# Summing a21 + a22 in two transfers, and moving four second-layer steps, in a Mamba-2 + ELU kernel

## The chip, the cores and the metric

The kernel runs on one core of a Trainium2 chip. The metric is the time of one execution on the device, in microseconds (us). A core has a matrix engine (TensorE, PE in the profile; PEld is its loading of weights), a vector engine (VectorE, DVE), a scalar engine (ScalarE, ACT), GpSimd (POOL) and a queue that issues transfers (SyncE, SP). Each runs its own list of instructions in order, and they wait for one another by semaphores. Transfers (DMAs) are issued by SP, ACT or POOL and run beside the engines. TensorE writes its products to PSUM, eight banks; DVE and ACT read them there.

## What is computed

A Mamba-2 scan over x (4 batches, 8 heads, 768 tokens, head dimension 32; state 16), and behind it a two-layer network with ELU, over 4 x 768 = 3072 tokens of 8 x 32 = 256 features:

```python
for c in range(nc):                       # chunks of tokens
    L = np.exp(cum[..., :, None] - cum[..., None, :]) * causal
    y_intra = np.einsum('bhij,bhjd->bhid', CB * L, xc)
    y_inter = np.einsum('bhin,bhnd->bhid', Cc, state) * decay_to_i[..., None]
    y[:, :, sl] = y_intra + y_inter
    state = decay_full[..., None, None] * state + np.sum(Bx, axis=2)
...
x = attn_out.transpose(0, 2, 1, 3).reshape(3072, 256)
h = x @ w_in                              # w_in 256 x 2048
g = np.where(h > 0, h, np.exp(np.minimum(h, 0)) - 1)
return g @ w_out                          # w_out 2048 x 256
```

The weights come as 64-bit floats, and the kernel turns them into 32-bit ones on the chip.

## The kernel before

**Tiles.** The tokens are cut into twelve blocks n = 0 to 11 of 256 tokens, taken in pairs (n, n + 1), so that a first-layer matmul has 512 columns. While the network runs on one pair, the scan of the next pair is put between its matmuls. The order on every engine is the one in which the program is written.

**First layer.** For the pairs from n = 2 on (n = 2 for its second half alone) `l1_words` (L778) computes a group m = 0 to 15 of 128 of the 2048 hidden features. It makes six matmuls in two PSUM banks, `high` and `both`. ACT then scales `both` (L796), DVE joins the two (L799), ACT takes the two functions of ELU (L805, L806), and DVE writes g with `end_words` (L813), which is called one group later. For every even m a subtraction on POOL follows. `high` is free only behind L813, `both` behind L796. `words_of_w` (L732) and `low_of_w` (L742) make from piece p of w_in the factors that groups 2p and 2p + 1 multiply by: the first on ACT and DVE, the second by two subtractions on POOL.

**Second layer.** The first blocks, 0 and 1, multiply plainly (`l2`, L825, matmuls at L832): step j reads the rows 2j and 2j + 1 (of 128 features) of w_out. From the pair 2 on, `second` (L871) multiplies two blocks together by seven products for four (the scheme of Strassen and Winograd). For this the features of w_out are taken in twos, even and odd, and its columns in two halves: a11, a12 (the even and the odd rows, columns 0 to 127), a21 and a22 (the same, columns 128 to 255) are views of w_out, each with eight rows i. Four sums of them are made beforehand: s1 = a21 + a22 in place of a21, and s2, s3, s4 in `s_out`. `less` (L709) writes the negative of a view on ACT, `plus` (L713) adds one to another by an adding transfer, which POOL issues (L715). The sum at issue is s1, written over a21, and it can start only when `l2` has read the last of a21.

`second(n)` is a generator. It goes twice (`half` 0 and 1, rows i = 0 to 3 and 4 to 7 of each view) through the seven products with a11, a12, s1, s2, s3, a22, s4, each of four *steps*, one row i a step, so that steps 0 to 27 are half 0 and steps 28 to 55 half 1. The k-th product of all fourteen goes into the one bank of the pool `p_o` if k is even, and into one of the seven banks of the pool `p_a` if it is odd; `p_a` also holds the first layer's and the scan's products. Behind the last step of a product ACT or DVE read it and free the bank: behind step 3 (a11) ACT copies it to p1 (L919), behind step 19 (s3) DVE adds it twice and ACT copies it to c12 (L944), behind step 27 (s4) DVE subtracts (L959). Behind step 31 DVE makes three adds (L885) and POOL four subtractions.

**The first pair with `second`.** The loop at L1309 begins with n = 4: its sixteen groups k are each followed by some scan work (`stage_scan`) and by a number of steps of `second(2)`, by a table at L1331:

```python
l2s((3 + (n == 4), 3 - (n == 4), 3, 3, 3, 3, 3, 3, 4, 5, 2, 2, 3, 1, 1, 0)[k])
```

So for n = 4 the groups 0 to 9 have 4, 2, 3, 3, 3, 3, 3, 3, 4 and 5 steps behind them. Steps 8 (the first with s1) and 24 (the first with s4) are the last of group 2 and the first of group 8. Behind the steps of group 9 come `scores` (L545, four banks of `p_a`), `sums` (L575, two banks), on DVE the weighing of the scores (L554), and two more steps; then `states` (DVE and POOL). Ahead of this loop, at L1277, stand the last preparations of w_in and w_out.

Of the kernel before, what the change touches and what calls it, by code (L numbers as in the profile page):

```python
# [14 lines left out]
ALU = mybir.AluOpType  # L15
# [17 lines left out]
def kernel(  # L33
# [27 lines left out]
    nc = tc.nc  # L61
# [30 lines left out]
    for k in range(4):  # L92
        (nc.scalar if k % 2 else nc.sync).dma_start(
            out=la0[BH * k:BH * (k + 1)],
            in_=a.rearrange("b h (c s) -> (b h) c s", s=P)[:, 0:2, :])
# [187 lines left out]
    for v in range(2):  # L283
        nc.gpsimd.affine_select(
            out=low16[Q * v:Q * v + Q], in_=low16[Q * v:Q * v + Q], pattern=[[1, Q]],
# [5 lines left out]
        out=hmask, in_=hmask, pattern=[[-N, NH]], compare_op=ALU.is_ge, fill=0.0,  # L291
        base=0, channel_multiplier=1)
    nc.gpsimd.affine_select(
        out=hmask, in_=hmask, pattern=[[N, NH]], compare_op=ALU.is_ge, fill=0.0,
# [8 lines left out]
        out=minus, in0=ident, scalar1=-1.0, scalar2=None, op0=ALU.mult)  # L303
# [213 lines left out]
    def decay(n, q):  # L517

        decay_of(n, 2 * q)
        decay_of(n, 2 * q + 1)  # L520
# [15 lines left out]
    def scores(*ns):  # L536

        gs = [psum([P, len(ns), 2, 2, Q], "ps_g") for _ in range(4)]
        for at, n in enumerate(ns):
            s = st[n]  # L540
            for u in range(2):
                for v in range(2):
                    for q in range(4):
                        rows, toks = slice(32 * q, 32 * q + 32), slice(Q * v, Q * v + Q)
                        nc.tensor.matmul(  # L545
                            out=gs[q][toks, at, u], lhsT=s["bt"][rows, u, toks],
                            rhs=s["ctm"][rows, u, :, toks], start=True, stop=True,
                            tile_position=(32 * q, Q * v), skip_group_check=True)
            s["g"], s["M"] = [g[:, at] for g in gs], []
# [160 lines left out]

        nc.scalar.activation(out, in_, ACT.Copy, scale=-1.0)

    def plus(out, in_):  # L713

        nc.gpsimd.dma_start(out=out, in_=in_, accum_op=ALU.add)  # L715

    def weight_sums():
        return [conv.tile([P, MC // 2, P], F32, tag="w64", name="w_sum", bufs=W_AHEAD)
# [3 lines left out]
    a_out = [w_parts[:, k, r] for r in range(2) for k in range(2)]  # L722
# [19 lines left out]
    def low_of_w(i):  # L742

        w0 = conv.tile([P, KC, CW], F32R, tag="w_in", name="w0", bufs=DF // CW + 1)
        for k in range(KC):
            sub(w0[:, k], pieces[i][0][:, k], k_words[i][:, 0, k].bitcast(F32))
        k_words[i] = k_words[i], w0
# [20 lines left out]
    def both_of_y(n):  # L768
        y = yT[n // 2].rearrange("p k b u i -> p k (b u i)")
        y1, y0 = y_words[n]  # L770
        both = ffn.tile([P, KC, 2 * BLK], F32R, tag="yT", name="y_both")
        for k in range(KC):
            nc.vector.scalar_tensor_tensor(
                out=both[:, k], in0=y1[:, k].bitcast(F32), scalar=1.0 - WORD,
                in1=y[:, k], op0=ALU.mult, op1=ALU.add)
        y_words[n] = y1, y0, both

    def l1_words(n, m, between=None):  # L778

        cols = slice(m % 2 * P, (m % 2 + 1) * P)  # L780
        w, w0 = k_words[m // 2]
        w1, both_w, w0 = w[:, 0, :, cols], w[:, 1, :, cols], w0[:, :, cols]
        y1, y0, both_y = y_words[n]
        high, both = psum([P, 2 * BLK], "ps_h"), psum([P, 2 * BLK], "ps_w")
        passes = [(high, w1, y1), (high, w0, y0), (both, both_w, both_y)]
        for ps, lhs, rhs in passes if m == (8 if n == 2 else 0) or m == 15 else passes[2:] + passes[:2]:
            for k in range(KC):
                nc.tensor.matmul(  # L788
                    out=ps, lhsT=lhs[:, k], rhs=rhs[:, k], start=k == 0 and lhs is not w0,
                    stop=k == KC - 1 and lhs is not w1)  # L790
        if between:
            words_of_y(between)
            if between == 4:
                both_of_y(4)
        e = ffn.tile([P, 2 * BLK], F32, tag="e", name="e", bufs=2)
        nc.scalar.activation(e, both, ACT.Copy, scale=WORD)  # L796
        if late:
            end_words()
        nc.vector.scalar_tensor_tensor(  # L799
            out=high, in0=high, scalar=WORD - 1.0, in1=e, op0=ALU.mult, op1=ALU.add)  # L800
        late.append((n, m, high, e))

    def begin_end():
        high, e = late[-1][2:]
        nc.scalar.activation(e, high, ACT.Relu, scale=-1.0)  # L805
        nc.scalar.activation(e, e, ACT.Exp, scale=-1.0)  # L806
# [3 lines left out]
    def end_words():  # L810
        n, m, h, e = late.pop(0)
        g_of[n, m] = ffn.tile([P, 2, BLK], F32, tag=f"g{m % 2}", name="g", bufs=12)
        nc.vector.scalar_tensor_tensor(  # L813
            out=g_of[n, m].rearrange("p b i -> p (b i)"), in0=e, scalar=1.0, in1=h,
            op0=ALU.subtract, op1=ALU.max)
        if m % 2 == 0 and (n, m) != (2, 14):
            sub(g_of[n, m][:, 1], g_of[n, m][:, 1], g_of[n, m][:, 0])
# [29 lines left out]
    def sub(out, in0, in1):  # L847
        nc.gpsimd.tensor_tensor(out=out, in0=in0, in1=in1, op=ALU.subtract)  # L848
# [113 lines left out]
    def store(n, at):  # L962
        r0 = row_of(n + at)
        nc.sync.dma_start(
            out=out[r0:r0 + BLK, :].rearrange("(t p) e -> p t e", p=P),
            in_=c_of[n][:, at].rearrange("p t e c -> p t (e c)"))
# [173 lines left out]
    def weigh_two(m, q):  # L1140
        weigh(m, q)
        weigh(m + 1, q)
# [17 lines left out]
    def turn_step(n, k, late):  # L1160
        m = n + 2
        if m == NP or k > 7:
            return
        if m == 6:
            steps = [(6, 2), (7, 0), None, (7, 1), None, (7, 2), (6, 3), (7, 3)]
            if steps[k // 2 * 2 + late]:
                turn_part(*steps[k // 2 * 2 + late])
        else:
            at = k // 2 * 2 + late
            turn_part(*[(m, 0), (m, 1), (m, 2), (m + 1, 0), (m + 1, 1), (m + 1, 2), (m, 3), (m + 1, 3)][at])  # L1170

    for j in range(2 * DIRECT):
        n, i = 2 + j // DIRECT, j % DIRECT
# [47 lines left out]
        if j == 6:  # L1221
            less(s_out[1], a_out[2])
            plus(s_out[1], a_out[0])
# [3 lines left out]
    for j in range(8, 16):  # L1227
# [46 lines left out]
        if i == 2:  # L1274
            less(s_out[0], s_out[1])
            plus(s_out[0], a_out[3])
    end_words()  # L1277
    for p in (1, 2):
        low_of_w(p)
    plus(a_out[2], a_out[3])  # L1280
    plus(s_out[2], a_out[1])
    words_of_w(3)
    decay(6, 0)
# [4 lines left out]
    def stage_scan(n, k):  # L1288

        m = n + 2  # L1290
        if k < 2:
            spread_exp(m + k)
        if k == 2:
            load_x(m)
            load_x(m + 1)
        heads = ((5 + 3 * k) // 2, (8 + 3 * k) // 2) if n == 4 else (2 * k - 2, 2 * k)
        for h in range(*heads) if 0 < k < 9 else ():
            decay_of(m + h // NH, h % NH)
        if k == 7:
            scaled(m, nc.gpsimd)  # L1300
            scaled(m + 1, nc.gpsimd)
        if k in (6, 7) and m + 2 < NP:
            load_bc(m + k - 4)
        if k == 10 and m + 2 < NP:
            for to in (m + 2, m + 3):
                load_b(to)
                spread_cum(to)

    for n in range(4, NP, 2):  # L1309
        m = n + 2 if n + 2 < NP else None  # L1310
        steps = second(n - 2)

        def l2s(count):
            for _ in range(count):
                next(steps)

        for k in range(16):
            l1_words(n, k, between=m if k == 15 else None)
            turn_step(n, k // 2 * 2 + 1, k % 2)
            if n == 4 and k == 0:  # L1320
                decay(6, 1)
            if m:
                stage_scan(n, k)
            begin_end()
            if k == 0 and n > 4:
                store(n - 4, 0)
                store(n - 4, 1)
            if not m:
                l2s(4 if k % 2 else 3)
                continue  # L1330
            l2s((3 + (n == 4), 3 - (n == 4), 3, 3, 3, 3, 3, 3, 4, 5, 2, 2, 3, 1, 1, 0)[k])  # L1331
            if k == 9:
                scores(m, m + 1)
                sums(m, m + 1)
                for q in range(4):
                    weigh_two(m, q)
                l2s(2)
                states(m)
            if k == 10:
                states(m + 1)  # L1340
            if k == 13:
                y = across(m, m + 1)
                inside(y, m, m + 1, ts=(0,))
                l2s(4)
                inside(y, m, m + 1, ts=(1,))
        if m:
            l2s(4)
            both_of_y(m)
        end_words()
        for _ in steps:  # L1350
            pass
    n = NP - 2
# [34 lines left out]
```

## Time and profile before

| | us |
|---|---|
| median of three runs | 349.99 (348.40 to 350.48) |
| the profiled execution | 349.12 |
| its span, first to last instruction | 347.4 |
| mean granted TensorE clock | 1.000 |

The profile shows one execution. A line of a timeline gives the start, the time taken, the engine, the line of the kernel, the operation, the tile written and the tiles read, their shapes, how many instructions were merged, and in brackets how long the engine idled before it and what ended that. A line of the waits gives who waited for whom, the sum in us, how often, and the longest. A line of the stretches gives from and to, the length, the busy time and number of instructions of PE, PEld, DVE, ACT and POOL, the granted clock, the share of the DMA engines and GB/s. Matmuls overlap and their ends are modelled, so that a row of them may reach past the start of the next.

### The profile page before, as it was taken

To read this page: it belongs to the slowest core of one execution; us is meant where nothing else is said; L and a number is where in the kernel's file an instruction comes from. 1 tells how busy PE (TensorE), PEld (TensorE's weight loads), DVE (VectorE), ACT (ScalarE), POOL (GpSimd) and SP (SyncE) were. 2 spreads that over 40 slices of the span, in tenths; PEclk is the share of its full clock that TensorE was granted. 3 is DMA by queue.
4 is the path that set the end of the run, shared out by engine and by line. 5 is a ranking of instruction groups with operands and counts; after the bars stand their busy time and mean duration, and the time that the engine had idled before them with its cause. 6 is when DMAs were issued, how large, how long until landed. Compare 5 with 4: busy or idle time off the path is not lost.

```text
span 347.4 us, 9861 instructions
## 1 busy us (share of the span) xinstructions
PE 340.3 (98%) x3878; PEld 298.2 (86%) x3878; DVE 253.7 (73%) x504; ACT 237.8 (68%) x541; POOL 214.2 (62%) x320
## 2 busy tenths in 40 slices
PE   8999999999999999999999999999999999999996
PEld 5669888888788889888999988989988999999996
DVE  3898988879898778875878675878675766665232
ACT  4789989599758898657699447699457566565000
POOL 5553554559987798864296764196754264455760
PEclk9999999999999999999999999999999999999999
DMA  8898998371793891070431070320000100001001
GB/s 149 219 232 167 312 193 222 78 145 44 117 153 68 121 142 43 10 160 4 106 62 32 10 159 5 101 37 3 2 0 4 63 0 3 0 2 58 4 1 61
DMA packets 76887, 28.58 MB, mean 82 GB/s; under 512 B 57833, under 2 KB 71721, under 8 KB 76841
## 3 DMA queue, kind: packets, MB, share of 16 engines
q1 hardware_dynamic: 70360, 25.60, 31.9%
q0 software_dynamic: 4160, 2.10, 5.6%
q8 instruction: 30, 0.49, 0.7%
q10 hardware_dynamic: 2320, 0.26, 0.5%
q14 instruction: 17, 0.13, 0.1%
HBM read 22.51 MB, written 3.34 MB: 74 GB/s over the span
## 4 chain that ended last, share of the span: by engine, by line
PE 78%; DMA 5%; ACT 5%; DVE 5%; SPq 3%; issue 2%; POOL 1%; DVEq 0%; POOLq 0%; ACTq 0%
PE ps_o L907 32%; PE ps_h L788 15%; PE ps_h L671 11%; PE ps_w L788 8%; PE ps_o L832 5%; DMA w_out<-w_out 3%; PE ps_y L638 2%; DMA w<-in_moe_w_in_dram 2%; DVE ps_h L799 1%; PE ps_g L545 1%; PE ps_y L620 1%; ACT e L806 1%; ACT e L805 1%; SPq L148 1%; PE ps_st L575 1%
## 5 line engine op out<-in xcount | busy, mean ns | idle before, releaser
L907 PEld LDWEIGHTS ps_o<-w_out,g 128*128 128x128 f32 x640 | 78.6, 191 | 4.4 <-ACT e L796 1.0
L907 PE MATMUL ps_o<-w_out,g 128*128 128x128 f32 x640 | 80.3, 275 | 0.8 <-DMA w_out<-w_out 0.8
L805 ACT ACTIVATE e<-ps_h 128x512 f32<-128x512 f32 x72 | 43.0, 597 | 50.0 <-DVE ps_h L799 50.0
L813 DVE SCALAR_TENSOR_TENSOR g<-e,ps_h 128x512 f32<-128x512 f32 x72 | 49.3, 685 | 34.3 <-ACT e L806 33.9
L848 POOL TENSOR_TENSOR g<-g 128x256 f32<-128x256 f32 x36 | 28.4, 789 | 56.4 <-DVE g L813 56.1
L799 DVE SCALAR_TENSOR_TENSOR ps_h<-ps_h,e 128x512 f32<-128x512 f32 x72 | 50.1, 695 | 13.5 <-ACT e L796 10.6
L796 ACT ACTIVATE e<-ps_w 128x512 f32<-128x512 f32 x72 | 42.2, 586 | 13.7 <-PE ps_w L788 13.6
L788 PE MATMUL ps_w<-y_both,w_words 128*128 128x512 f32 x144 | 51.0, 434 | 0.0
L806 ACT ACTIVATE e<-e 128x512 f32<-128x512 f32 x72 | 45.5, 632 | 2.3
L671 PE MATMUL ps_h<-yT,w_in 128*128 128x256 f32 (+1 forms) x208 | 45.2, 368 | 1.4 <-POOL w_in L252 1.3
L788 PE MATMUL ps_h<-y,w_words 128*128 128x512 f32 x144 | 46.2, 402 | 0.0
L788 PE MATMUL ps_h<-y,w 128*128 128x512 f32 x144 | 44.8, 392 | 0.0
L671 PEld LDWEIGHTS ps_h<-yT,w_in 128*128 128x128 f32 x208 | 36.3, 190 | 7.5 <-POOL w_in L252 2.8
L525 ACT ACTIVATE L<-L,ncum 128x64 f32<-128x64 f32 x160 | 42.2, 336 | 0.2
L907 PE MATMUL ps_o<-w_sum,g 128*128 128x128 f32 x304 | 38.3, 275 | 0.0
L907 PEld LDWEIGHTS ps_o<-w_sum,g 128*128 128x128 f32 x304 | 37.1, 192 | 1.1
L530 POOL TENSOR_SCALAR_AFFINE_SELECT L<-L 64x512 f32<-64x512 f32 x40 | 29.6, 741 | 10.0 <-ACT L L525 8.6
L788 PEld LDWEIGHTS ps_h<-y,w 128*128 128x128 f32 x144 | 27.0, 188 | 6.7 <-POOL w L848 0.2
L848 POOL TENSOR_TENSOR g<-t,g 128x256 f32<-128x256 f32 x40 | 28.0, 734 | 5.8 <-PE ps_o L907 5.7
L788 PEld LDWEIGHTS ps_h<-y,w_words 128*128 128x128 f32 x144 | 26.4, 188 | 5.7 <-issue 0.4
L832 PE MATMUL ps_o<-w_out,g 128*128 128x256 f32 x128 | 31.0, 384 | 0.0
L848 POOL TENSOR_TENSOR t<-g 128x256 f32<-128x256 f32 x40 | 29.0, 757 | 0.2
(131 smaller groups left out, 536.0 us busy)
## 6 DMA issues: line engine op xcount, KB each, us to landing
L<-flat SPq DMA_DIRECT2D x20, 256.0 KB
w<-in_moe_w_out_dram SPq DMA_DIRECT2D x8, 512.0 KB
w<-in_moe_w_in_dram SPq DMA_DIRECT2D x7, 512.0 KB
xr<-in_x_dram SPq DMA_DIRECT2D x24, 128.0 KB
out_dram<-c_sum SPq DMA_DIRECT2D x9, 256.0 KB
bc<-in_B_dram SPq DMA_DIRECT2D x24, 64.0 KB
w_sum<-w_out POOLq DMA_DIRECT2D x3, 512.0 KB, 9.4
bc<-in_C_dram SPq DMA_DIRECT2D x22, 64.0 KB
```

The lines of the kernel that those rows point to most:

```text
L525: nc.scalar.activation(L[:, h, u], L[:, h, u], ACT.Exp, bias=ncum[:, u, row:row + 1])
L530: nc.gpsimd.affine_select(out=part, in_=part, pattern=[[0, 4], [0, 2], [1, Q]], compare_op=ALU.is_ge, fill=0.0, base=0, channel_multiplier=-1)
L671: nc.tensor.matmul(out=ps[:, j, toks], lhsT=w_in[i][:, k, j * P:(j + 1) * P], rhs=yT[n // 2][:, k, n % 2].rearrange("p u i -> p (u i)")[:, ...
L788: nc.tensor.matmul(out=ps, lhsT=lhs[:, k], rhs=rhs[:, k], start=k == 0 and lhs is not w0, stop=k == KC - 1 and lhs is not w1)
L796: nc.scalar.activation(e, both, ACT.Copy, scale=WORD)
L799: nc.vector.scalar_tensor_tensor(out=high, in0=high, scalar=WORD - 1.0, in1=e, op0=ALU.mult, op1=ALU.add)
L805: nc.scalar.activation(e, high, ACT.Relu, scale=-1.0)
L806: nc.scalar.activation(e, e, ACT.Exp, scale=-1.0)
L813: nc.vector.scalar_tensor_tensor(out=g_of[n, m].rearrange("p b i -> p (b i)"), in0=e, scalar=1.0, in1=h, op0=ALU.subtract, op1=ALU.max)
L832: nc.tensor.matmul(out=o_of[n][:, ts], lhsT=g_of[n, j][:, m % 2, ts * P:(ts + 1) * P], rhs=w_out[:, m], start=(m == 0 and ts == 0), stop=( ...
L848: nc.gpsimd.tensor_tensor(out=out, in0=in0, in1=in1, op=ALU.subtract)
L907: nc.tensor.matmul(out=ps[:, ts], lhsT=b[:, ts * P:(ts + 1) * P], rhs=a[:, i], start=(i == chunk[0] and ts == 0), stop=(i == chunk[-1]), s ...
```

## The change

The one transfer for s1 becomes two, over rows 0 to 3 and over rows 4 to 7 of the views. The first is issued between `low_of_w(1)` and `low_of_w(2)`, the second behind `low_of_w(2)`, where the whole one stood. And in the table of steps, for n = 4 alone, group 8 gets eight steps instead of four and group 9 one instead of five: steps 28 to 31 now come ahead of group 9's passes.

```diff
-    def plus(out, in_):
+    def plus(out, in_, rows=slice(None)):
 
-        nc.gpsimd.dma_start(out=out, in_=in_, accum_op=ALU.add)
+        nc.gpsimd.dma_start(out=out[:, rows], in_=in_[:, rows], accum_op=ALU.add)
...
     end_words()
-    for p in (1, 2):
-        low_of_w(p)
-    plus(a_out[2], a_out[3])
+    low_of_w(1)
+    plus(a_out[2], a_out[3], slice(0, 4))
+    low_of_w(2)
+    plus(a_out[2], a_out[3], slice(4, 8))
     plus(s_out[2], a_out[1])
...
-            l2s((3 + (n == 4), 3 - (n == 4), 3, 3, 3, 3, 3, 3, 4, 5, 2, 2, 3, 1, 1, 0)[k])
+            l2s((3 + (n == 4), 3 - (n == 4), 3, 3, 3, 3, 3, 3, 4 + 4 * (n == 4), 5 - 4 * (n == 4),
+                 2, 2, 3, 1, 1, 0)[k])
```

## The prediction

> **What bounds the kernel now.** I read the page's busy line first, then the list of who waited for whom on TensorE, then the shares of two stretches, then the timelines of the engines between 106 and 149 us. The times below are those of the profiled execution: 349.12 us, of which 347.4 are its span and 1.72 lie around it. It is 0.87 us under the median of the three other runs (349.99); the mean of the four is 349.50.
>
> ```profile
> span 347.4 us, 9861 instructions
> PE 340.3 (98%) x3878; PEld 298.2 (86%) x3878; DVE 253.7 (73%) x504; ACT 237.8 (68%) x541; POOL 214.2 (62%) x320
> ```
> ```profile
> PE ps_o L907 <- DMA w_out<-w_out: 0.8, 1, 0.8
> PE ps_st L575 <- DVE c_sum L885: 0.4, 1, 0.4
> ```
> ```profile
> 113.00:146.00 33.00, 31.76 (x323) 28.16 (x321) 25.37 (x46) 28.30 (x69) 29.33 (x39) 1.00 0.52 81
> 146.00:200.00 54.00, 54.00 (x650) 48.75 (x637) 41.38 (x86) 38.23 (x90) 33.56 (x53) 1.00 0.29 62
> ```
>
> TensorE (PE) is busy 98% of the span at a granted clock of 1.00, and from 146 to 200 us it has no gap, nor does its list of waits show one later: what reaches it there is paid in full, and what is won before 146 us is kept to the end. In the stretch of the first pair, 113 to 146 us, it idles 33.00 - 31.76 = 1.24 us, and the list names two waits there, 0.8 and 0.4 us. These are the two that the edits touch, so nothing in the profile offers this change more than some 1.5 us.
>
> ```profile
> 115.10 1.95 PE L907 MATMUL ps_o<-w_out,g 128*128 128x128 f32 x16
> ...
> 120.57 1.05 PE L907 MATMUL ps_o<-w_out,g 128*128 128x128 f32 x8
> 122.42 0.68 PE L907 MATMUL ps_o<-w_out,g 128*128 128x128 f32 x4 [0.80 <-DMA w_out<-w_out]
> ...
> 137.97 1.95 PE L907 MATMUL ps_o<-w_sum,g 128*128 128x128 f32 x16
> 139.67 0.70 PE L788 MATMUL ps_w<-y_both,w_words 128*128 128x512 f32 x2
> ...
> 141.14 2.39 PE L907 MATMUL ps_o<-w_out,g 128*128 128x128 f32 x20
> 143.46 1.21 PE L545 MATMUL ps_g<-ctm,bct 32*64 32x128 f32 x64
> 144.59 0.32 PE L575 MATMUL ps_st<-xr,b_tok 64*32 64x64 f32 x8
> 145.32 0.84 PE L575 MATMUL ps_st<-xr,b_tok 64*32 64x64 f32 x56 [0.41 <-DVE c_sum L885]
> 146.09 1.16 PE L907 MATMUL ps_o<-w_out,g 128*128 128x128 f32 x8
> ```
> ```profile
> 120.33 1.09 PEld L907 LDWEIGHTS ps_o<-w_out,g 128*128 128x128 f32 x8
> 122.39 0.52 PEld L907 LDWEIGHTS ps_o<-w_out,g 128*128 128x128 f32 x4 [0.96 <-ACT e L796]
> ...
> 137.74 1.99 PEld L907 LDWEIGHTS ps_o<-w_sum,g 128*128 128x128 f32 x16
> ...
> 145.29 0.71 PEld L575 LDWEIGHTS ps_st<-xr,b_tok 64*32 64x32 f32 x56 [0.54 <-PE ps_g L545]
> ```
>
> A step of the second layer is four rows of L907, about 0.45 us (five steps from 141.14 to 143.46). The first wait stands in front of step 8, the first that multiplies by a21+a22. The second stands in front of the state sums, in group 9.
>
> **The first transfer: what goes.** GpSimd (POOL) issues the one transfer now at 113.01:
>
> ```profile
> 106.53 1.81 POOL L848 TENSOR_TENSOR w<-w_in,w_words 128x256 fp32r<-128x256 f32 x2
> 110.21 2.13 POOL L848 TENSOR_TENSOR w<-w_in,w_words 128x256 fp32r<-128x256 f32 x2 [1.87 <-ACT w_words L737]
> 113.01 1.56 POOL L715 DMA_DIRECT2D w_out<-w_out  x1 [0.67 <-PE ps_o L832]
> 115.45 1.54 POOL L715 DMA_DIRECT2D w_sum<-w_out  x1 [0.88 <-DVE g L813]
> ```
> ```profile
> 96.45 1.89 PE L832 MATMUL ps_o<-w_out,g 128*128 128x256 f32 x8
> ```
> ```profile
> w_out<-w_out POOLq DMA_DIRECT2D x1, 512.0 KB, 9.3
> ```
> ```profile
> DMA to landing us min/median/max: 8.4/9.4/10.5
> ```
>
> It waits for the last L832 matmuls, which read the rows 6 and 7 of what it overwrites. The first half overwrites rows 0 to 3; they are last read by l2(1, 3), whose eight rows end at 96.45 + 1.89 = 98.34. So it issues right behind low_of_w(1), at 106.53 + 1.81 = 108.34. Its issue costs POOL something up to the 1.56 of a whole one (half as many pieces, so 0.8 is the lower end); POOL idles 1.87 us there, and 1.56 fits. Were that cover gone, low_of_w(2) and the two transfers behind it would move by up to 1.56, partly taken up by the idle 0.67 and 0.88 behind them. No row shows a transfer of 256 KB: it lands between half of 8.4 and the whole 10.5 after issue, so at 112.5 to 118.8; I take 6. Step 8 wants it at 121.4, so the value does not matter. By the fit of the Trainium skill, "DMA: Bandwidth & Descriptors", section on the anatomy of an SWDGE transfer (some 2.0 us fixed plus the bytes over 436 GB/s), an estimate for the half is 2.6 us and for the whole 3.2; the measured 9.3 is three times that, and the sum comes out the same by either.
>
> The second half keeps the old start, since it has the old wait, and lands no later than the old 122.3 by more than the first half's issue can push it; its reader is the third product of the second half, behind 146 us.
>
> **What is late next.** With the transfer in place, step 8 waits for the bank it writes, the only one of its pool, which ScalarE (ACT) empties with the copy of p1; and later step 24 waits for the same bank, which ACT empties with the copy of c12 (L944):
>
> ```profile
> 121.17 0.35 ACT L919 COPY p_sum<-ps_o 128x256 f32<-128x256 f32 x1
> ...
> 142.69 0.58 ACT L796 ACTIVATE e<-ps_w 128x512 f32<-128x512 f32 x1
> ```
> ```profile
> 136.85 0.34 DVE c_sum L885
> ...
> 137.27 0.37 ACT c_sum L944
> ```
>
> From the end of a VectorE (DVE) add (144.43 + 0.75 = 145.18, row below) to the weight load that it releases (145.29) it takes 0.11. The p1 copy ends at 121.52, so step 8's weights load at 121.63 instead of 122.39: TensorE gains 0.76. It then leads by 0.76 for six groups. ACT and DVE do not get earlier with it, for they wait for each other and not for TensorE: from 105 to 160 us ACT has one such wait, and that is of group 10, behind 145.
>
> ```profile
> ACT e L796 <- PE ps_w L788: 2.3, 1, 2.3
> ```
> The c12 copy still ends at 137.64. Step 24's weights load at 137.75 or later, where they load now at 137.74, and its first matmul, behind no other, at about 137.78 against 137.97. Of the lead of 0.76, 0.57 is lost there and 0.19 is left. This is the step on which my forecast turns.
>
> **The four moved steps.** Steps 28 to 31 go ahead of group 9's passes. They carry no DMA. On DVE their three adds, which free a bank, come ahead of L813 of group 8 and L799 of group 9; on POOL four subtractions come ahead of one of L813's.
>
> ```profile
> 141.40 0.41 DVE L959 TENSOR_TENSOR c_sum<-ps_o,c_sum 128x256 f32<-128x256 f32 x1
> 142.89 0.69 DVE L813 SCALAR_TENSOR_TENSOR g<-e,ps_h 128x512 f32<-128x512 f32 x1 [1.07 <-ACT e L806]
> 143.49 0.69 DVE L799 SCALAR_TENSOR_TENSOR ps_h<-ps_h,e 128x512 f32<-128x512 f32 x1
> 144.09 0.41 DVE L885 TENSOR_TENSOR p_sum<-ps_o,c_sum 128x256 f32<-128x256 f32 x1
> 144.43 0.75 DVE L885 TENSOR_TENSOR c_sum<-ps_o,c_sum 128x256 f32<-128x256 f32 x2
> 145.09 2.73 DVE L554 TENSOR_TENSOR M<-ps_g,L 128x256 f32<-128x256 f32 x8
> ...
> 148.90 0.68 DVE L813 SCALAR_TENSOR_TENSOR g<-e,ps_h 128x512 f32<-128x512 f32 x1
> ```
> ```profile
> 144.44 2.79 POOL L848 TENSOR_TENSOR g<-t,g 128x256 f32<-128x256 f32 x4
> ```
>
> TensorE afterwards: eight steps from 137.78 take 139.67 - 137.97 = 1.70 for four and 4/5 of 143.46 - 141.14, 1.86, for four, so to 141.34; the passes of group 9 take 141.14 - 139.67 = 1.47, to 142.81; one step 0.46, to 143.27; the scores 144.59 - 143.46 = 1.13, to 144.40. DVE ends L959 at 141.81 and does the three adds (145.18 - 144.09 = 1.09) in the 1.07 us that it idles now, to 142.90; L813 of group 8 starts at 142.89 now, so it is not pushed. The banks of scores and sums are then free by 142.90 (the adds), 142.69 + 0.58 = 143.27 (L796) and 142.89 + 0.69 = 143.58 (L813). The scores may wait 0.06 for the second; the sums, from 144.40 on, for none. They take 146.09 - 145.32 = 0.77 for 56 and 0.11 for 8, so to 145.28, and with the 0.06 to 145.34. Now it is 146.09: the gain is 0.75 us. POOL's four subtractions lie in its own slack: the subtraction that they delay by 2.79 is of g that only the next pair reads.
>
> The second wait is 0.54 by the weight loads and 0.41 by the matmuls. The Trainium skill, "Trainium Kernel Development and Optimization", section Performance Expectations, calls matmul busy time a bad measure, because matmuls are pipelined. The trace agrees, the first wait being 0.96 by the one and 0.80 by the other; by the matmul rows alone the sum would be 0.19 + 0.41 = 0.60 us.
>
> **The rivals.** *Both waits are won whole.* If the c12 copy came earlier with TensorE, the lead would hold: 0.76 + 0.54 = 1.3 us, so 348.2. Against it: the copy hangs on a DVE add at 136.85, not on TensorE. 0.10.
>
> *The first transfer is not sooner*, because it is made to wait for all reads of w_out: POOL would stand from 108.34 to 113.01 and low_of_w(2) with it, which is read only in group 4, after 125 us. Then only the 0.54 remains: 349.0. Against it: the matmuls at 115.10, steps 0 to 3, read other columns of w_out while the transfer into it was under way, with no wait. 0.08.
>
> *Slower: a worse bank for group 10.* The moved steps change in which order the seven banks are given out. Now group 10 gets the banks of the first scores, free two weighings (2 x 0.34) into the row at 145.09. If it got the bank of group 9's high product, free only behind L813 at 148.90 + 0.68 = 149.58, some 0.5 earlier then, TensorE, there two steps behind the sums, at some 146.2, would stand 2.9 us, net +2.15: 351.65. It decides from the point where a bank is freed behind 146.2. For it: the pool has no free bank there. Against: banks are given out in the order in which they come free. 0.08.
>
> *The reordering gives back what it wins*: TensorE ends step 31 later than 141.8, so the adds push L813, L799 and the weighing; the gain is 0 to 0.3, so 349.4. For it: the margin of L813 is nil. 0.10.
>
> **The numbers.** The forecast, 0.64, is 349.12 - 0.75 = 348.37 against the profiled execution, and 348.75 against the mean of the four times, which I predict. The runs before lie 1.1 under and 1.0 over their mean, so the range takes in 1.5 us (the two waits, 0.96 + 0.54) below that mean and half a us of scatter, 347.5, and above it no gain with 1.0 of scatter, 350.5; the bank rival is mostly left out. One per cent, 3.5 us, is about what a measurement of this kernel can tell from no change. Every case above lies within it; the scatter and what I overlook get 0.06 for faster and 0.05 for slower.
>
> **What would show it.** Right: the wait for the DMA is gone from TensorE's list and in its place stands one of about 0.6 us at L907 for ACT's copy at L944; the wait at L575 for c_sum is gone; two issues of 256 KB, the first at 108.3 us; the third step of group 2 starts at 121.6, the state sums end at 145.3. Wrong: L944 starts before 137; any new wait at L545 or at L788 of group 10; POOL idle from 108 to 113.

## The result, and the profile after

| | before | after |
|---|---|---|
| median of 22 runs each, us | 349.34 (348.31 to 351.24) | 348.56 (347.96 to 349.99) |
| the span of the profiled execution, us | 347.4 | 347.0 |
| mean granted TensorE clock | 1.000 | 1.000 |

The ratio after to before is 0.9973 (0.9962 to 0.9984): the change is worth 0.94 us (0.56 to 1.33), by the two medians 0.78. The forecast was 348.75 us, a gain of 0.75.

The page's busy line of the kernel after, then the one line of TensorE's list of waits that belongs to the first pair, then the two stretches:

```profile
span 347.0 us, 9862 instructions
...
PE 340.6 (98%) x3878; PEld 298.0 (86%) x3878; DVE 253.9 (73%) x504; ACT 237.9 (69%) x541; POOL 215.2 (62%) x321
```
```profile
PE ps_o L907 <- ACT c_sum L944: 0.4, 1, 0.4
```
```profile
113.00:146.00 33.00, 32.61 (x328) 28.67 (x328) 26.12 (x48) 28.30 (x69) 29.15 (x39) 1.00 0.44 73
146.00:200.00 54.00, 54.00 (x637) 48.55 (x637) 41.46 (x87) 38.56 (x90) 33.57 (x54) 1.00 0.29 61
```

Both waits of before are gone, the one for the DMA and the one for DVE's adds. One has come in their place, at L907 for ACT's copy of c12 (L944). TensorE idles 33.00 - 32.61 = 0.39 us in the first pair where it idled 1.24: 0.85 us less. The profiled execution was taken on another launch, in which all that lies ahead of the first pair came some 0.3 us later (the first passes of group 0 start at 113.51, before at 113.22). So from here on I count from that row. The timeline of TensorE, and below it of its weight loads, in the kernel after:

```profile
113.51 0.81 PE L788 MATMUL ps_h<-y,w_words 128*128 128x512 f32 x2
...
120.80 1.75 PE L907 MATMUL ps_o<-w_out,g 128*128 128x128 f32 x12
...
137.96 2.05 PE L907 MATMUL ps_o<-w_sum,g 128*128 128x128 f32 x16 [0.39 <-ACT c_sum L944]
139.84 1.95 PE L907 MATMUL ps_o<-w_out,g 128*128 128x128 f32 x16
...
143.56 1.21 PE L545 MATMUL ps_g<-ctm,bct 32*64 32x128 f32 x64
144.70 0.86 PE L575 MATMUL ps_st<-xr,b_tok 64*32 64x64 f32 x64
145.49 1.16 PE L907 MATMUL ps_o<-w_out,g 128*128 128x128 f32 x8
```
```profile
121.84 0.52 PEld L907 LDWEIGHTS ps_o<-w_out,g 128*128 128x128 f32 x4 [0.18 <-ACT p_sum L919]
...
137.95 1.86 PEld L907 LDWEIGHTS ps_o<-w_sum,g 128*128 128x128 f32 x16 [0.82 <-ACT c_sum L944]
```

The three steps of group 2 are one row of twelve matmuls now (120.80); before, the third stood apart, behind the wait. The eight steps of group 8 begin with a wait. Scores, sums and the step behind them follow one another without one. That last step starts 145.49 - 113.51 = 31.98 us behind the first passes, where it took 146.09 - 113.22 = 32.87. I call this stretch the *mark*; it is 0.89 us shorter.

The queue of POOL, and how long the two halves took from issue to landing:

```profile
106.81 1.79 POOL L848 TENSOR_TENSOR w<-w_in,w_words 128x256 fp32r<-128x256 f32 x2
108.18 1.68 POOL L715 DMA_DIRECT2D w_out<-w_out  x1
110.50 2.12 POOL L848 TENSOR_TENSOR w<-w_in,w_words 128x256 fp32r<-128x256 f32 x2 [0.64 <-ACT w_words L737]
113.30 1.29 POOL L715 DMA_DIRECT2D w_out<-w_out  x1 [0.69 <-PE ps_o L832]
115.74 1.55 POOL L715 DMA_DIRECT2D w_sum<-w_out  x1 [1.16 <-DVE g L813]
```
```profile
DMA to landing us min/median/max: 4.6/4.6/4.6
...
DMA to landing us min/median/max: 5.8/5.8/5.8
```

The first half goes out at 108.18 and waits for none of the later reads of w_out; it has landed at 112.8, and step 8's weights load at 121.84. Its issue takes 1.68 us of the 1.87 that POOL idled there.

DVE, around the moved steps, in the kernel after:

```profile
141.67 0.41 DVE L959 TENSOR_TENSOR c_sum<-ps_o,c_sum 128x256 f32<-128x256 f32 x1
142.00 0.41 DVE L885 TENSOR_TENSOR p_sum<-ps_o,c_sum 128x256 f32<-128x256 f32 x1
142.33 0.75 DVE L885 TENSOR_TENSOR c_sum<-ps_o,c_sum 128x256 f32<-128x256 f32 x2
143.16 0.69 DVE L813 SCALAR_TENSOR_TENSOR g<-e,ps_h 128x512 f32<-128x512 f32 x1
```

The three adds fill the 1.07 us that DVE idled in ahead of L813, and L813 has no wait to speak of behind them.

Not all of the 0.89 us reaches the end. In the next pair, before and after:

```profile
168.38 0.62 PE L788 MATMUL ps_w<-y_both,w_words 128*128 128x512 f32 x2
168.84 1.50 PE L907 MATMUL ps_o<-w_out,g 128*128 128x128 f32 x12
170.10 0.71 PE L788 MATMUL ps_w<-y_both,w_words 128*128 128x512 f32 x2
```
```profile
167.81 0.74 PE L788 MATMUL ps_w<-y_both,w_words 128*128 128x512 f32 x2
168.38 1.50 PE L907 MATMUL ps_o<-w_out,g 128*128 128x128 f32 x12
169.64 0.70 PE L788 MATMUL ps_w<-y_both,w_words 128*128 128x512 f32 x2
```
```profile
168.05 0.19 PEld L788 LDWEIGHTS ps_w<-y_both,w_words 128*128 128x128 f32 x1 [0.27 <-DVE y_both L773]
```

The three rows took 170.10 - 168.38 = 1.72 us and take 169.64 - 167.81 = 1.83: TensorE is here so early that a weight load waits for DVE's y_both (L773). Of the 0.89 us 0.11 goes there. The last row of matmuls of the whole kernel starts 342.25 - 113.22 = 229.03 us behind the first passes before and 341.77 - 113.51 = 228.26 after, so 0.77 is left at the end.

### The profile page after: what moved, and what is told of

Same layout as the page of the kernel before. It is cut to its first block, busy times and chain, and to the rows that moved or that the text cites. A ratio compares the mean times of both kernels' runs of the same rounds, so it can differ in the third digit from the quotient of the medians.

```text
span 347.0 us, 9862 instructions
## 1 busy us (share of the span) xinstructions
PE 340.6 (98%) x3878; PEld 298.0 (86%) x3878; DVE 253.9 (73%) x504; ACT 237.9 (69%) x541; POOL 215.2 (62%) x321
## 4 chain that ended last, share of the span: by engine, by line
PE 87%; SPq 3%; ACT 3%; DMA 3%; DVE 2%; issue 1%; POOL 0%; DVEq 0%; ACTq 0%
PE ps_o L907 34%; PE ps_h L788 18%; PE ps_h L671 10%; PE ps_w L788 9%; PE ps_o L832 8%; PE ps_y L638 3%; DMA w<-in_moe_w_in_dram 2%; PE ps_g L545 2%; PE ps_y L620 2%; PE ps_st L575 1%; SPq L148 1%; DMA bc<-in_B_dram 1%; SPq L179 1%; DVE ps_h L799 1%; SPq L116 1%
## 5 line engine op out<-in xcount | busy, mean ns | idle before, releaser
L907 PEld LDWEIGHTS ps_o<-w_out,g 128*128 128x128 f32 x640 | 78.7, 191 | 3.6 <-ACT p_sum L919 0.2
L907 PE MATMUL ps_o<-w_out,g 128*128 128x128 f32 x640 | 80.5, 275 | 0.0
L805 ACT ACTIVATE e<-ps_h 128x512 f32<-128x512 f32 x72 | 43.0, 597 | 50.4 <-DVE ps_h L799 50.4
L813 DVE SCALAR_TENSOR_TENSOR g<-e,ps_h 128x512 f32<-128x512 f32 x72 | 49.4, 686 | 33.4 <-ACT e L806 33.0
L799 DVE SCALAR_TENSOR_TENSOR ps_h<-ps_h,e 128x512 f32<-128x512 f32 x72 | 50.1, 695 | 13.3 <-ACT e L796 8.3
L788 PE MATMUL ps_w<-y_both,w_words 128*128 128x512 f32 x144 | 51.2, 435 | 0.0
L796 ACT ACTIVATE e<-ps_w 128x512 f32<-128x512 f32 x72 | 42.2, 586 | 12.7 <-PE ps_w L788 12.6
L806 ACT ACTIVATE e<-e 128x512 f32<-128x512 f32 x72 | 45.5, 632 | 2.3
L788 PE MATMUL ps_h<-y,w_words 128*128 128x512 f32 x144 | 46.3, 403 | 0.0
L788 PE MATMUL ps_h<-y,w 128*128 128x512 f32 x144 | 44.8, 392 | 0.0
L525 ACT ACTIVATE L<-L,ncum 128x64 f32<-128x64 f32 x160 | 42.2, 336 | 0.2
L907 PE MATMUL ps_o<-w_sum,g 128*128 128x128 f32 x304 | 38.4, 275 | 0.4 <-ACT c_sum L944 0.4
L907 PEld LDWEIGHTS ps_o<-w_sum,g 128*128 128x128 f32 x304 | 37.0, 192 | 1.8 <-ACT c_sum L944 0.8
L788 PEld LDWEIGHTS ps_h<-y,w 128*128 128x128 f32 x144 | 27.0, 188 | 6.7 <-POOL w L848 0.2
L788 PEld LDWEIGHTS ps_h<-y,w_words 128*128 128x128 f32 x144 | 26.4, 188 | 5.7 <-issue 0.4
```

The costliest lines, as they stand in the source:

```text
L525: nc.scalar.activation(L[:, h, u], L[:, h, u], ACT.Exp, bias=ncum[:, u, row:row + 1])
L788: nc.tensor.matmul(out=ps, lhsT=lhs[:, k], rhs=rhs[:, k], start=k == 0 and lhs is not w0, stop=k == KC - 1 and lhs is not w1)
L799: nc.vector.scalar_tensor_tensor(out=high, in0=high, scalar=WORD - 1.0, in1=e, op0=ALU.mult, op1=ALU.add)
L813: nc.vector.scalar_tensor_tensor(out=g_of[n, m].rearrange("p b i -> p (b i)"), in0=e, scalar=1.0, in1=h, op0=ALU.subtract, op1=ALU.max)
L907: nc.tensor.matmul(out=ps[:, ts], lhsT=b[:, ts * P:(ts + 1) * P], rhs=a[:, i], start=(i == chunk[0] and ts == 0), stop=(i == chunk[-1]), s ...
```

## The experiments

A difference of half a microsecond is no more than the intervals of most runs below, so each kernel is judged by its trace, and its time stands beside. Two profiled executions of the kernel after gave marks of 31.98 and 31.97 us. All times in this table are us from the first row of L788 at some 113 us, to the first row of the passes of group 3, of step 24, of the scores (L545), and of the step behind the state sums (the mark); the last column is the ratio of times to the kernel before. The mark ends at some 145 us, and not all of what is won there reaches the end. In the executions of E3 and E4 the second row of L638 (in the scan, at 157.96 and 159.35 us) took 1.05 and 1.14 us to the next row, where it takes 0.79 in the kernel after: TensorE paused there for nothing that the profile shows. In E11, the same kernel as E3, it took 0.78, so this differs between executions; why stays open.

| kernel | group 3 | step 24 | scores | mark | ratio (95%) |
|---|---|---|---|---|---|
| before | 9.64 | 24.75 | 30.24 | 32.87 | 1 |
| after | 8.80 | 24.45 | 30.05 | 31.98 | 0.9973 (0.9962 to 0.9984) |
| E1: transfers alone | 8.78 | 24.42 | 30.03 | 32.82 | 0.9987 (0.9963 to 1.0012) |
| E2: steps alone | 9.52 | 24.57 | 30.06 | 31.98 | 0.9980 (0.9949 to 1.0012) |
| E3: after, other bank | 8.80 | 23.82 | 29.30 | 31.57 | 0.9952 (0.9930 to 0.9975) |
| E4: both halves late | 8.82 | 24.47 | 30.07 | 32.00 | 0.9972 (0.9948 to 0.9995) |
| E5: steps and bank | 9.50 | 24.52 | 30.00 | 31.93 | 0.9993 (0.9959 to 1.0027) |
| E6: transfers and bank | 8.81 | 23.91 | 29.41 | 32.88 | 1.0027 (1.0011 to 1.0043) |
| E7: transfer later | | | | 37.57 | 1.0172 (1.0148 to 1.0196) |
| E8: less work on ACT | 8.80 | 24.25 | 29.85 | 31.77 | 0.9970 (0.9943 to 0.9997) |
| E9: shorter ring | 8.78 | 23.89 | 29.39 | 31.31 | 0.9964 (0.9944 to 0.9984) |
| E10: after, once more | 8.80 | 24.45 | 30.04 | 31.97 | 0.9972 (0.9955 to 0.9989) |
| E11: E3, once more | 8.78 | 23.81 | 29.29 | 31.56 | 0.9966 (0.9949 to 0.9983) |

### E1 and E2: one part each

E1 is the kernel after with the old table of steps, E2 the kernel before with the new one (both shown against the kernel after; in E2 `plus` has no rows either):

```diff
-            l2s((3 + (n == 4), 3 - (n == 4), 3, 3, 3, 3, 3, 3, 4 + 4 * (n == 4), 5 - 4 * (n == 4),
-                 2, 2, 3, 1, 1, 0)[k])
+            l2s((3 + (n == 4), 3 - (n == 4), 3, 3, 3, 3, 3, 3, 4, 5, 2, 2, 3, 1, 1, 0)[k])
```
```diff
-    low_of_w(1)
-    plus(a_out[2], a_out[3], slice(0, 4))
-    low_of_w(2)
-    plus(a_out[2], a_out[3], slice(4, 8))
+    for p in (1, 2):
+        low_of_w(p)
+    plus(a_out[2], a_out[3])
```

> Only the two transfers, the steps as before. The mark is the time from the first passes of group 0 to the first step behind the state sums: 113.22 to 146.09, 32.87 us, before; 113.51 to 145.49, 31.98, after. Theory A (ACT and DVE set the end of this stretch: TensorE's lead from the earlier transfer is lost at the copy of c12, and what is left of it at the state sums): no wait for the transfer, a wait of about 0.8 us at step 24 by the weight loads and one of 0.7 to 0.9 at the state sums, and the mark stays at 32.8 to 32.9; time as before within 0.1 us. Rival B (the two waits are worth their rows one by one): the mark falls by 0.8 to 32.1 and the time by 0.8 us, 0.23 per cent.

> Only the four moved steps, the one transfer as before. Theory A: the wait for the transfer stays at 0.8 to 0.96 us, the one at the state sums is gone, step 24 does not wait, and the mark falls by about 0.6 us, from 32.87 to 32.25; time 0.6 us lower, 0.17 per cent. Rival B: it falls by the 0.41 of the matmul row or the 0.54 of the weight loads, to 32.35 to 32.45. Rival C (only the two edits together do anything): 32.87.

E1's TensorE, at the sums:

```profile
143.39 1.21 PE L545 MATMUL ps_g<-ctm,bct 32*64 32x128 f32 x64
144.53 0.32 PE L575 MATMUL ps_st<-xr,b_tok 64*32 64x64 f32 x8
145.41 0.84 PE L575 MATMUL ps_st<-xr,b_tok 64*32 64x64 f32 x56 [0.56 <-DVE c_sum L885]
146.18 1.16 PE L907 MATMUL ps_o<-w_out,g 128*128 128x128 f32 x8
```

E1 reaches group 3 with a lead of 9.64 - 8.78 = 0.86 us, step 24 with 0.33, the scores with 0.21, and the step behind the sums with 0.05: the wait for DVE's adds has grown from 0.41 to 0.56 and takes the rest. DVE did not come earlier, so whoever arrives earlier waits longer.

E2's TensorE, at step 8 and at the sums:

```profile
122.28 0.68 PE L907 MATMUL ps_o<-w_out,g 128*128 128x128 f32 x4 [0.74 <-DMA w_out<-w_out]
...
144.38 0.86 PE L575 MATMUL ps_st<-xr,b_tok 64*32 64x64 f32 x64
145.17 1.16 PE L907 MATMUL ps_o<-w_out,g 128*128 128x128 f32 x8
```

E2 keeps the wait for the DMA (0.90 in its weight loads) and has the whole mark of the kernel after, 31.98. The kernel after leads E2 by 0.72 at group 3, by 0.12 at step 24, and by 0.01 at the scores. So beside the moved steps the transfers bring nothing that shows in the mark. The steps alone do not bring all of the 0.89 either: E2 leads the kernel before by 24.75 - 24.57 = 0.18 at step 24 already, up to which the two run the same instructions. That much differs between executions; from step 24 on E2 wins 0.89 - 0.18 = 0.71, and this is the steps' share.

### E3, E5, E6: is it the bank that eats the lead?

The product of steps 24 to 27 goes into a bank of the pool of seven instead of the one that ACT must empty first (E3 on the kernel after, E5 on E2, E6 on E1):

```diff
-                pool, tag = (p_a, "a") if (7 * half + r) % 2 else (p_o, "o")
+                many = (7 * half + r) % 2 or (n == 2 and half == 0 and r == 6)
+                pool, tag = (p_a, "a") if many else (p_o, "o")
```

> The kernel after, with the product of steps 24 to 27 of the first pair in one of the seven banks, so that step 24 does not wait for the copy of c12. Theory A: the wait of 0.82 at step 24 (by the weight loads) is gone, TensorE keeps its whole lead of 0.83 up to the scores and waits there some 0.3 to 0.4 us for the bank that DVE's three adds free at 142.9 of the profile before; the mark falls by 0.25 to 0.3, from 31.98 to 31.7. Rival B: the lead is kept to the end, the mark is 31.4. Rival C (the copy of c12 was not what cost the lead): no change, 31.98.

> The moved steps and step 24's product in another bank, but the one transfer as before. The mark (first passes of group 0 to the first step behind the state sums) was 32.87 us before, 31.98 after, 31.98 with the moved steps alone and 31.57 with all three. Theory A (the early transfer buys a lead, and only the other bank lets TensorE keep it): here there is no lead to keep, the wait for the transfer stays at 0.7 to 0.9 us, and the mark stays at 31.9 to 32.0. Rival B (the other bank by itself is what made the 0.4 us): 31.57.

> The two transfers and step 24's product in another bank, the steps as before. Theory A (the end of the stretch is set by the three adds behind step 31, which stand behind L813 and L799 in VectorE's list): no wait for the transfer and none at step 24, but the lead of 0.8 us is all lost at the state sums, which wait 1.2 to 1.4 us by the weight loads, and the mark stays at 32.8 to 32.9. Rival B (a lead that is not lost at step 24 is kept): 32.0.

E3's TensorE at step 24 and at the scores:

```profile
136.50 1.95 PE L908 MATMUL ps_o<-w_sum,g 128*128 128x128 f32 x16
...
141.98 1.55 PE L545 MATMUL ps_g<-ctm,bct 32*64 32x128 f32 x64
```
```profile
142.36 0.94 PEld L545 LDWEIGHTS ps_g<-ctm,bct 32*64 32x64 f32 x58 [0.18 <-issue]
```

The wait at step 24 is gone, and step 24 comes 24.45 - 23.82 = 0.63 us sooner than in the kernel after. Of this 0.41 is left in the mark. The rest goes inside the scores, whose 64 matmuls take 1.55 us instead of 1.21. Six of them load at once, the other 58 from 142.36 on; DVE's three adds, which free a bank, end at 142.24 in E3. The trace names no releaser here, so that it is this bank is inferred from the 0.12 between the two (0.11 in the prediction's row). The lead is 0.75 still at the scores (30.05 - 29.30), and 0.41 behind them: more than the 0.25 to 0.3 that theory A gave, and less than rival B's 0.6.

The marks of the four kernels with the moved steps show how the parts depend on each other. Without the bank the transfers bring 31.98 - 31.98 = 0, with it 31.93 - 31.57 = 0.36; the bank brings 0.05 without the transfers and 0.41 with them. And without the moved steps the two together bring nothing (E6, 32.88): its lead of 0.83 at the scores ends in a wait there for ACT (0.26) and one at the sums for DVE's adds (0.59). A wait taken away is worth what the next wait lets through.

E6 was measured slower than before by 0.4 to 1.5 us, though its mark and its span (347.4 us) are those of before. Over all executions of the same rounds the medians of the spans are 347.6 and 347.5 us, and what lies outside the span is 2.11 us against 1.85. So by the medians about half of the difference stands ahead of the first instruction or behind the last; why stays open. E5's ratio is hardly below 1 and its range is wide; by the medians of the same rounds it is 348.60 against 349.23 us.

### E4 and E7: does the start of the transfer matter?

E4 issues both halves where the whole one stood, one behind the other. E7 is E2 with the whole transfer behind the one of s_out:

```diff
     low_of_w(1)
-    plus(a_out[2], a_out[3], slice(0, 4))
     low_of_w(2)
+    plus(a_out[2], a_out[3], slice(0, 4))
     plus(a_out[2], a_out[3], slice(4, 8))
```
```diff
-    plus(a_out[2], a_out[3])
     plus(s_out[2], a_out[1])
+    plus(a_out[2], a_out[3])
```

> The kernel after, with both halves of the transfer behind low_of_w(2), so that the first is issued no sooner than the whole one was (about 113.0 us). Theory A: a half lands 4.6 to 5.8 us after its issue, at about 119, and step 8 wants it at 121.5: no wait, the mark is that of after, 31.98. Rival B (the sooner start is what counts, a half takes nearly as long as a whole): step 8 waits some 0.8 us and the mark is about 32.25, that of the moved steps alone.

> The moved steps alone, with the one transfer behind that of s_out[2], so that it is issued at about 117.0 instead of 113.0 us and lands at 126.3 to 127.5. Theory A (TensorE has no slack for being late, though an early transfer gains it nothing): step 8 waits 4.8 to 6 us by the weight loads instead of 0.9, nothing of the 4 to 5 us more is taken up later, and the mark rises from 31.98 to 36 to 37; time 4 to 5 us, 1.1 to 1.5 per cent, over the moved steps alone. Rival B (since ACT and DVE run some 3 us behind TensorE there, a part of it is absorbed): the mark is 33 to 34.5.

E4 issues the first half at 112.68, 4.5 us later than the kernel after, and it lands 4.3 us after its issue, at 117.0; step 8 wants it at some 121.9. (The second, queued behind it, lands 7.8 us after its own.) Every column of its row in the table is that of the kernel after, within 0.02. So to take the wait away it was enough to halve the transfer; that the first half starts sooner changes nothing.

E7's TensorE around step 8, and short stretches of it:

```profile
127.00 1.20 PE L907 MATMUL ps_o<-w_out,g 128*128 128x128 f32 x4 [4.95 <-ACT e L805]
127.85 1.20 PE L788 MATMUL ps_w<-y_both,w_words 128*128 128x512 f32 x2
128.84 1.05 PE L788 MATMUL ps_h<-y,w_words 128*128 128x512 f32 x2
...
130.26 1.50 PE L907 MATMUL ps_o<-w_out,g 128*128 128x128 f32 x12
```
```profile
126.00:128.00 2.00, 1.00 (x5) 1.03 (x6) 1.22 (x3) 1.70 (x4) 2.00 (x4) 0.63 1.10 168
128.00:130.00 2.00, 2.00 (x6) 1.61 (x6) 1.18 (x3) 1.97 (x7) 2.00 (x4) 0.52 0.25 75
130.00:132.00 2.00, 2.00 (x16) 1.88 (x15) 1.82 (x4) 1.59 (x5) 2.00 (x4) 1.00 0.17 51
```

The wait names ACT's L805, which had long been done; what came at 126.8 was the transfer, issued at 116.8 and 10.0 us on its way. The wait has grown by some 4.2 us against E2's 0.7, and the mark by 37.57 - 31.98 = 5.59. The 1.4 us over that are in the granted clock, the column behind POOL's: 0.63 and 0.52 in the two stretches from 126 to 130 us. The share that is missing, 0.37 x 2 + 0.48 x 2 = 1.70 us, is that of 3.4 us at half clock. In stretches of half a us the clock is 1.00 up to 126.5, 0.50 from there to 129.5 and 0.59 in the next. The first 0.5 us at half clock thus fall into the wait and cost nothing; the other 2.9 cost half of it, 1.45 us. The passes of group 3 show it: 1.20 and 1.05 us where such a row takes 0.71 and 0.62. The Trainium skill, "TensorE: Matmul & The Clock Gate", Part 1, says that the gate halves the clock after an idle window of some 3.4 us and gives it back after one that is busy. By that rule a wait under 3.4 us costs no clock, and one of 5 us can cost one window at half. The trace agrees, as far as its waits go: those of 0.4 to 1.0 us in the other kernels left the clock at 1.00, and that of 5 us brought 3.4 us at half. No run here has a wait between.

### E8 and E9: what sets the copy that step 24 waits for?

The copy of c12 stands on ACT's list, among the activations of the first layer and the exponentials of the decays (L525). Is ACT too full, or is it the order in which ACT and DVE wait for each other? E8 is the kernel after without the sixteen exponentials of block 7; ten of them, some 2.4 us, stand ahead of the copy. E9 is the kernel after without L806 (the second function of ELU) in groups 2 to 5 of the first pair, about 4 x 0.53 = 2.1 us of ACT's work (from the start of such a row to the next).

```diff
-        for u in range(2):
+        for u in range(2 if n != 7 else 0):
```
```diff
+        if late[-1][0] == 4 and late[-1][1] in (2, 3, 4, 5):
+            return
```

> The kernel after, without the sixteen exponentials of the decays of block 7 on ACT in groups 4 to 8 (they are left out, so that block 7 is computed with the logarithms in their place). Ten of them, 2.4 us, stand ahead of the copy of c12. Theory A (the pace of ACT and DVE sets when c12 is copied): the copy comes 0.8 us or more earlier against the first passes, the wait at step 24 is gone, the scores wait for no bank, and the mark falls from 31.98 to 31.1 to 31.5. Rival B (something else holds step 24 or the scores): 31.8 to 32.0.

> The kernel after, without the second function of ELU on ACT (L806) in groups 2 to 5 of the first pair, four instructions, 2.5 us, left out so that these groups come out without the exponential. Theory A2 (not ACT's load sets when c12 is copied, but the ring L796, L799, L805, L806 of a group, each of which waits for the one before, at 2.62 us a group; the decays lie in its shadow): the copy comes 2.0 to 2.5 us earlier against the first passes than the 24.02 of after, so at 21.5 to 22.0; the wait at step 24 is gone, the scores wait for no bank, and the mark falls from 31.98 to 31.4 or 31.5. Rival A (ACT's load counts, in whichever instruction) would have shown the same with the decays left out, where the copy came 0.18 earlier. Rival B (neither): the copy stays within 0.3 of 24.0 and the mark at 31.8 to 32.0.

ACT in the kernel after, in E8 and in E9 (the line numbers of E9 from L806 on are two higher):

```profile
133.55 0.60 ACT L805 ACTIVATE e<-ps_h 128x512 f32<-128x512 f32 x1 [0.41 <-DVE ps_h L799]
...
136.19 0.60 ACT L805 ACTIVATE e<-ps_h 128x512 f32<-128x512 f32 x1
136.82 0.63 ACT L806 ACTIVATE e<-e 128x512 f32<-128x512 f32 x1
137.53 0.37 ACT L944 COPY c_sum<-ps_o 128x256 f32<-128x256 f32 x1
```
```profile
133.59 0.60 ACT L805 ACTIVATE e<-ps_h 128x512 f32<-128x512 f32 x1 [0.88 <-DVE ps_h L799]
...
136.22 0.60 ACT L805 ACTIVATE e<-ps_h 128x512 f32<-128x512 f32 x1 [0.88 <-DVE ps_h L799]
...
137.39 0.35 ACT L944 COPY c_sum<-ps_o 128x256 f32<-128x256 f32 x1
```
```profile
127.83 0.60 ACT L805 ACTIVATE e<-ps_h 128x512 f32<-128x512 f32 x1 [0.41 <-DVE ps_h L799]
...
131.82 0.60 ACT L805 ACTIVATE e<-ps_h 128x512 f32<-128x512 f32 x1 [0.41 <-DVE ps_h L799]
...
135.51 0.35 ACT L946 COPY c_sum<-ps_o 128x256 f32<-128x256 f32 x1
```

From group to group L805 comes every 136.19 - 133.55 = 2.64 us in the kernel after, and every 2.63 in E8: ACT spent what it was spared on waiting for DVE's L799, 0.88 us a group. The copy starts 24.02 us behind the first passes in the one and 23.84 in the other, 0.18 sooner for 2.4 us of work, where E8's theory A had 0.8 or more. In E9 L805 comes every 2.00 us (two groups from 127.83 to 131.82, 3.99) and the copy 21.80 behind the first passes, 2.22 sooner for 2.1 us of work. So it is not ACT's load. It is a ring: L796 on ACT, L799 on DVE, L805 and L806 on ACT, then L796 of the next group. What stands in the ring moves the copy, and what stands in its gaps hardly does. At 2.63 us a group it is hardly faster than TensorE (one group of passes with three steps took 2.73), so it makes up only some 0.1 us of its delay a group.

In E9 no wait for another engine stands between step 8 and the mark, and the mark is 31.31: 1.56 us less than before, about what the two waits of before came to (0.96 + 0.54 = 1.50 in the weight loads).

### E10 and E11: the kernel after and E3 side by side

> The kernel after once more, for a direct comparison on one chip with step 24's product in another bank. All theories: mark 31.9 to 32.0, wait of 0.8 us at step 24 by the weight loads, time 0.25 per cent under before.

> The kernel after with the product of steps 24 to 27 of the first pair in one of the seven banks, once more. Theory A: mark 31.55 to 31.7, no wait at step 24, time 0.4 us under the kernel after, so some 0.1 per cent, and 0.35 per cent under before. Rival: no different from after.

By the marks E3's kernel beats the kernel after by 0.41 us both times (31.57 against 31.98, 31.56 against 31.97). By the medians of the same rounds it is 348.54 against 348.67 us, which the intervals do not tell apart. At the last row of matmuls of the whole kernel it is less: E3 and E11 stand there 228.02 and 227.83 us behind the first passes, the kernel after 228.26 and 228.30, and E2, with the steps alone, 228.07. E3's is the best complete kernel by the mark; how much of that reaches the end these runs do not settle.

## Why the prediction was right, and where its terms were off

**What bounds the kernel** held: TensorE has no gap from 146 to 200 us before or after, and what the first pair won arrived at the end, but for the 0.11 us at y_both (and the pause at L638 in E3 and E4). The prediction had that wait nowhere. "What is won before 146 us is kept to the end" was too strong: a stretch without gaps shows that nothing is late for TensorE as it comes now, not how much sooner it could come.

**The transfer.** The first issue came at 108.18 (said: 108.34), ahead of low_of_w(2), and hid in POOL's idle time. The halves landed 4.6 and 5.8 us after issue (said: 6, between 4.2 and 10.5). By the fit of the Trainium skill, "DMA: Bandwidth & Descriptors", section on the anatomy of an SWDGE transfer, an estimate was 2.6 us; for these adding transfers the measurement decides against it. Step 8's weights wait for the p1 copy, as said: they load at 121.84, which less the 0.29 us by which this execution is late is 121.55 (said: 121.6); the sums end at 145.20 in the same count (said: 145.3).

**The lead is lost at step 24.** This was the step on which the forecast turned, and it is shown, by the wait for L944 that came, by E3, where it goes with the bank, and by E8 and E9, where only the ring moves it. "They wait for each other and not for TensorE" was the reason given, and E9 is its test. The reading behind it missed a line: from 105 to 160 us ACT's list of waits for TensorE has two, not one.

```profile
ACT ob L838 <- PE ps_o L832: 1.0, 1, 1.0
```

This one ends at 113.61, ahead of step 8 and of the lead, so that the argument loses nothing by it. The size is in part luck: a lead of 0.76 with 0.57 lost and 0.19 left was forecast. Against the profiled execution of before it was 0.84 at group 3, 0.30 at step 24, and 0.19 at the scores. But E2, with the transfer as before, stands within 0.01 of the kernel after at the scores. What the transfers alone are worth is thus 0 to 0.2, and the executions of the same old transfer differ by nearly that much (9.64, 9.52 and 9.50 at group 3), so that the 0.19 came out as said proves little. One thing was not foreseen: the sixteen matmuls behind the wait took 2.05 us and not 1.95, so that a lead in the start of step 24 (0.12 over E2) is gone by the scores.

**The moved steps** were taken as worth 0.56 from step 24 to the mark (8.12 to 7.56); with step 24 unstalled, in E2, it was 8.12 - 7.41 = 0.71. The step that was mis-sized is the sums: I put 0.77 for 56 matmuls behind 0.11 for 8, from rows between which the engine had stalled, and 0.06 for a bank of the scores. Unbroken, the 64 took 145.49 - 144.70 = 0.79 instead of 0.88, and the scores waited for no bank. The three errors, 0.09 and 0.06 too little here, and 0.11 too much for what comes behind, nearly cancel in the time, and that is luck: the mark fell by 0.89 where 0.75 was said, and 0.77 was left at the end.

**The choice of measure.** The rule that the prediction quotes is about how near a kernel comes to the peak, not about what a wait costs. The weight loads put the second wait at 0.54 and the matmuls at 0.41. From the first matmul of the sums to the next step it was 146.09 - 144.59 = 1.50 us with the wait and 0.79 without: 0.71 lay there. Neither wait told it; the distance between starts did.

**The rivals.** That both waits are won whole did not happen, and E9 shows what it would have taken, a ring that is shorter by L806 in four groups. That the first transfer would stand for all reads of w_out is refuted by its issue at 108.18, that group 10 gets a worse bank by its passes, which follow two steps behind the sums with no wait, and that the reordering gives back its gain by DVE's row at 143.16. That a measurement tells no less than one per cent was too cautious: 22 executions of each kernel told 0.27 per cent from nothing.

## What to carry to other kernels

Before an early transfer is counted as a gain, follow the lead that it makes to the next place where the engine meets work of others: here a copy on ACT, then adds on DVE, each took what the one before had let through, and only all three edits together (transfer, steps, bank) kept most of it up to the mark. When an engine seems late, look for the ring of engines that wait for each other: work in the gaps of a ring costs little to keep and gives little when removed (here 0.18 us of 2.4). And measure a stall by the distance between the starts on both sides of it, against the same distance where it runs through, not by the idle time alone.

## What was not expected of the hardware

The issue on POOL of half a transfer is not half as long: 1.68 and 1.29 us in the kernel after for 256 KB each, 1.56 before for 512 KB.

A late operand cost more than its lateness once TensorE had stood for 5 us: E7 lost 1.4 us more to the clock. After a wait of 0.3 to 0.4 us at full clock step 24's row took 0.1 us longer, too (2.05 us in the kernel after, E1, E4 and E8, 1.95 without the wait).
